# One ordinary GpSimd instruction behind the last 64-bit add of a launch

## The chip, the cores and the metric

One core of one Trainium2 chip. The metric is the device time of a launch in microseconds (us). The profiled span, from the first to the last instruction, is 1.7 to 1.9 us shorter than the device time of the same launch. Engines: PE is TensorE, PEld its weight loads, DVE VectorE, ACT ScalarE, POOL GpSimd, SP SyncE; a q behind the name is the engine's sequencer, under which waits, branches and library loads stand in the profile. The granted clock is TensorE's clock as a share of full speed. The chain is the work that ended last, followed back from the last instruction to what released it. An ACTIVATE is one ScalarE instruction. L1447 is line 1447 of that kernel's source; the changed kernel has one line more above this place and two above the end, so L1447 of before is L1448 of after.

## The reference, cut to what matters

```python
def reference(A_x, A_wq, A_wk, A_wv, A_wo, B_x, B_wqkv, B_w_phi, B_wo):
    # A: softmax attention, 32 query heads of 16, one key and value head, sequence 2048
    q = heads(A_x @ A_wq);  k = A_x @ A_wk;  v = A_x @ A_wv
    a = merge(softmax(q @ k.T * 16 ** -0.5) @ v) @ A_wo
    # B: linear attention with a softmax feature map, 32 heads of 16
    ...
    return concatenate([a, b], axis=-1)          # (1, 2048, 1024) bf16
```

## The kernel before, in the parts that matter

A scheduler in Python lays out a fixed order of instructions for every engine ahead of the launch. About two thirds of the exponentials of part A are ScalarE activations (L1646; 700 instructions of 1024 columns). The others (648 of 512 columns) are made from bits: VectorE scales scores into 16-bit words (L1751), and GpSimd makes shifted copies of four such words at a time with 64-bit adds (L1781):

```python
fn = lambda g: g.int64_add(out=b, in0=a, in1=256 * t * 0x1000100010001)
```

The start of the launch, cut:

```python
add("pool", lambda g: g.memset(self.ones, 1.0), writes=["ones"])
add("pool", lambda g: g.memset(self.zero, 0.0), writes=["zero"])
self.fill((512,) * self.NWARM, start=True)            # 12 warm-up matmuls on TensorE
last = self.load_xT(self.A_x, self.xT, 0, "AxT", None)  # first transposed chunk of x
...                                                   # loads of wk_raw, wq, wv; x chunks 1 to 3
add("pool", lambda g: g.memset(half[:, 0:1], 0.0), writes=["half0"])
...                                                   # four memsets of 16 rows of half
add("pool", lambda e: e.tensor_scalar(out=half[:, 1:2], in0=half[:, 0:1], scalar1=-1.0, scalar2=0.25,
                                      op0=ALU.mult, op1=ALU.add), reads=hk, writes=["half1"])      # L1447
add("pool", lambda g: g.tensor_copy(out=wk_rep..., in_=srck), reads=["wk_raw"], writes=["wk_rep"]) # L1450
...                                                   # memsets; the identity (affine_select, L1465); masks
```

The K projection (L1535) is the first real work of TensorE. It needs wk_rep and the first chunk of x. All GpSimd instructions run in this order. No library load is written in the source: the build puts one ahead of the first instruction that needs another library than the one known to be loaded. At the beginning of a launch it takes none as loaded, so there is a load ahead of L1447 and another ahead of the first 64-bit add. In the profile a load is a pair of MODIFY_POOL_CONFIG.

## Time and profile before

| | before |
|---|---|
| device time, median of 4 runs | 720.66 us (719.64 to 720.98) |
| profiled span (of one more launch, 721.12 us) | 719.37 us |
| busy: PE, DVE, ACT, POOL | 95, 86, 95, 72% |
| idle POOL ahead of the first tensor_scalar | 9.00 us |
| first ACTIVATE | 17.30 us |

The page cuts the span into 40 slices of 18 us and gives each a digit, the busy share in tenths.

```profile
PE   6999999999999999999999999999999999999995
...
ACT  1999999999999999999999999999999999999992
```

From the second slice on both are full. The prediction shows the lines of the first one.

### The profile page before, as it was taken

Reading aid. Unit: us, or ns where it says so; the run is one execution under the profiler, and the core shown is the slowest. Engines: PE = TensorE matmul, PEld = TensorE weight load, DVE = VectorE, ACT = ScalarE, POOL = GpSimd, SP = SyncE. Lnnn points to the kernel's source line nnn. Section 1 sums busy time; section 2 is a strip of 40 time slices with the busy share of each in tenths; the row PEclk is TensorE's granted clock in tenths of the full one; section 3 lists DMA queues with packets and bytes.
Section 4 is the critical chain, followed back from the end, with each engine's and each line's share of the span. In section 5 each row is a group of like instructions: output and inputs, shape, how many; then the busy total and the mean of one; then the engine's idle time right before and its main releaser. Section 6 shows DMA issues by size and latency. Waiting matters only on the chain.

```text
span 719.4 us, 18224 instructions
## 1 busy us (share of the span) xinstructions
PE 681.1 (95%) x7548; PEld 211.5 (29%) x7548; DVE 620.6 (86%) x1039; ACT 683.9 (95%) x771; POOL 521.4 (72%) x521
## 2 busy tenths in 40 slices
PE   6999999999999999999999999999999999999995
PEld 2322222322322332332222322323332323333322
DVE  1788899999999999999888988898978989889974
ACT  1999999999999999999999999999999999999992
POOL 3188788777777677776778878587878787777870
PEclk8999999999999999999999999999999999999999
DMA  6502233111112101111011111011111211111212
GB/s 139 127 3 39 42 38 66 19 7 12 9 13 37 9 8 10 14 9 10 7 8 19 16 20 17 12 19 23 20 17 9 28 22 23 16 14 16 31 16 52
DMA packets 47890, 18.28 MB, mean 25 GB/s; under 512 B 38708, under 2 KB 45940, under 8 KB 47800
## 3 DMA queue, kind: packets, MB, share of 16 engines
q1 hardware_dynamic: 45400, 16.23, 17.5%
q8 instruction: 60, 0.98, 0.6%
q10 hardware_dynamic: 2400, 0.82, 0.5%
q14 instruction: 30, 0.25, 0.1%
HBM read 2.28 MB, written 4.19 MB: 9 GB/s over the span
## 4 chain that ended last, share of the span: by engine, by line
ACT 49%; PE 30%; DVE 17%; issue 2%; POOL 1%; DMA 1%; SPq 0%; ACTq 0%; DVEq 0%; POOLq 0%
ACT f_PT L1646 47%; PE f_ps L1591 10%; DVE f_Z L1751 9%; PE f_ps L1811 8%; PE f_ps L1693 3%; PE f_ps L2245 2%; PE f_ps L1581 2%; PE f_ps L1897 1%; DVE f_vS L2103 1%; ACT f_ET L2160 1%; DVE f_ssum L2069 1%; PE f_ps L2153 1%; PE f_ps L2055 1%; DVE f_On L1878 1%; ACT f_Ek L2063 1%
## 5 line engine op out<-in xcount | busy, mean ns | idle before, releaser
L1646 ACT ACTIVATE f_PT<-f_ps 128x1024 bf16<-128x1024 f32 x700 | 654.8, 1093 | 20.5 <-PE f_ps L1591 17.8
L1781 POOL INT64_ADD f_Z<-f_Z x486 | 512.6, 1055 | 167.5 <-DVE f_Z L1751 128.5
L1751 DVE TENSOR_SCALAR f_Z<-f_ps 128x512 int16<-128x512 f32 x648 | 425.6, 681 | 53.6 <-PE f_ps L1591 50.9
L1591 PE MATMUL f_ps<-f_QA,f_KR 32*128 32x512 bf16 x2048 | 280.2, 384 | 15.1 <-ACT f_PT L1646 11.5
L1811 PE MATMUL f_ps<-f_Z,f_VK 128*32 128x512 f16 x2592 | 227.5, 386 | 4.2 <-DVE f_Z L1751 1.6
L1591 PEld LDWEIGHTS f_ps<-f_QA,f_KR 32*128 32x128 bf16 x2048 | 70.4, 91 | 254.7 <-ACT f_PT L1646 224.9
L1693 PE MATMUL f_ps<-f_PT,f_VA 128*32 128x512 bf16 x1400 | 131.6, 385 | 0.1
L1811 PEld LDWEIGHTS f_ps<-f_Z,f_VK 128*32 128x32 bf16 x2592 | 56.4, 94 | 105.4 <-issue 61.0
L1693 PEld LDWEIGHTS f_ps<-f_PT,f_VA 128*32 128x32 bf16 x1400 | 33.5, 94 | 47.8 <-issue 44.9
L2215 DVE TENSOR_TENSOR f_Wk<-f_ps,f_wq 128x512 bf16<-128x512 f32 x32 | 21.8, 680 | 3.6 <-PE f_ps L2204 3.6
L1412 PE MATMUL f_ps<-f_ones,f_zero 128*128 128x512 bf16 (+4 forms) x112 | 20.7, 369 | 1.3 <-POOL f_zero L1431 1.3
L1418 DVE COPY f_accS<-f_ps 128x512 f32<-128x512 f32 x31 | 21.0, 677 | 0.0
L1543 DVE TENSOR_SCALAR f_KR<-f_ps,f_half 128x512 bf16<-128x512 f32 x8 | 5.7, 744 | 17.7 <-PE f_ps L1535 17.7
L2103 DVE TENSOR_TENSOR f_vS<-f_ps,f_rs 128x1024 bf16<-128x1024 f32 x16 | 19.7, 1229 | 0.3 <-PE f_ps L2093 0.2
L2069 DVE TENSOR_REDUCE f_ssum<-f_Ek 128x64 f32<-128x1024 bf16 x16 | 19.3, 1204 | 0.0
L2160 ACT ACTIVATE f_ET<-f_ps 128x512 bf16<-128x512 f32 x32 | 18.8, 689 | 0.1
L2063 ACT ACTIVATE f_Ek<-f_ps 128x512 bf16<-128x512 f32 x32 | 18.2, 655 | 0.0
L1581 PE MATMUL f_ps<-f_AxT,f_wq 128*128 128x512 bf16 x64 | 17.7, 406 | 0.0
L2153 PE MATMUL f_ps<-f_BxT,f_Wq 128*128 128x512 bf16 x64 | 16.6, 382 | 0.7 <-DVE f_Z L1751 0.7
L2245 PE MATMUL f_ps<-f_Bwo,f_oT 128*128 128x512 bf16 x64 | 16.6, 382 | 0.4 <-DVE f_QA L1418 0.2
L1418 DVE CAST f_outB<-f_ps 128x512 bf16<-128x512 f32 x16 | 10.9, 681 | 6.8 <-PE f_ps L2245 6.8
L2055 PE MATMUL f_ps<-f_Wk,f_BxT 128*128 128x512 bf16 x64 | 16.6, 382 | 0.0
(94 smaller groups left out, 296.8 us busy)
## 6 DMA issues: line engine op xcount, KB each, us to landing
f_denS<-f_denS SPq DMA_DIRECT2D x124, 30.0 KB, 3.0
out_dram<-f_outB SPq DMA_DIRECT2D x16, 128.0 KB, 2.0
f_denC<-f_accS SPq DMA_DIRECT2D x124, 2.0 KB, 1.7
f_denS<-f_denC SPq DMA_DIRECT2D x124, 2.0 KB, 1.7
out_dram<-f_outA SPq DMA_DIRECT2D x14, 128.0 KB, 2.6
f_On<-f_Ot SPq DMA_DIRECT2D x60, 16.0 KB, 1.8
f_Bwv<-in_B_wqkv_dram SPq DMA_DIRECT2D x1, 512.0 KB, 4.5
f_Bwo<-in_B_wo_dram SPq DMA_DIRECT2D x1, 512.0 KB, 6.3
```

Source lines behind the costliest of these rows:

```text
L1418: self.add("dve", lambda v: v.tensor_copy(out=out, in_=in_), reads=reads, writes=writes)
L1581: mm = pe.matmul(ps[:, bank, :], lhsT=self.wq[:, dc, A * 128:A * 128 + 128], rhs=xT[:, dc, qc * 512:(qc + 1) * 512], start=(dc == 0), stop ...
L1591: return pe.matmul(self.ps[:, bank, :], lhsT=self.KR[32 * g:32 * g + 32, sc % 2, kap * 128:(kap + 1) * 128], rhs=self.QA[32 * g:32 * g + 3 ...
L1646: self.add("act", lambda a: a.activation(out=PT[:, sl[0]:sl[0] + size, :], in_=ps[:, b0:b0 + size, :], func=ACT.Exp), reads=[("PS", b0 + i ...
L1693: mm = pe.matmul(ps[32 * g:32 * g + 32, bank, :], lhsT=VA[:, kap, :], rhs=PT[:, slots[g], :], start=start, stop=stop, tile_position=(0, 32 ...
L1751: self.add("dve", lambda v: v.tensor_scalar(out=o, in0=ps[:, bank, :], scalar1=self.Z1, scalar2=self.Z0, op0=ALU.mult, op1=ALU.add), reads ...
L1781: fn = lambda g: g.int64_add(out=b, in0=a, in1=256 * t * 0x1000100010001)
L1811: mm = pe.matmul(ps[32 * g:32 * g + 32, bank, :], lhsT=self.VK[:, t, kap, :], rhs=Zf[:, sl[g], :], start=start, stop=stop, tile_position=( ...
L2069: self.add("dve", lambda v: v.tensor_reduce(out=ssum[:, r, :], in_=Ek[:, r].rearrange("p a h f -> p (a h) f"), axis=AX.X, op=ALU.add), rea ...
L2103: self.add("dve", lambda v: v.tensor_tensor(out=vS[:, :, :, 0:16], in0=v3, in1=rs.unsqueeze(3).to_broadcast([128, 2, 32, 16]), op=ALU.mult ...
L2160: self.add("act", lambda e: e.activation(out=self.ET[:, sl, :], in_=self.ps[:, bank, :], func=ACT.Exp, scale=1.0 - 2.0 * a), reads=[("PS", ...
L2245: mm = pe.matmul(ps[:, bank, :], lhsT=oT[:, r, C, :], rhs=self.Bwo[:, C, :], start=(C == 0), stop=(C == 3))
```

## The change

Intent: the launch shall end with the ordinary library loaded, so that the next launch of the same kernel finds it and its first load has nothing to do.

```diff
         self.half = sb("half", [128, 2], F32)
+        self.pad = sb("pad", [128, 1], F32)
...
         self.run()
+        self.add("pool", lambda g: g.tensor_scalar(out=self.pad, in0=self.half[:, 0:1], scalar1=1.0, scalar2=None, op0=ALU.mult), reads=["half1"], writes=["pad"])
         self.finish_last()
```

## The prediction

> **What bounds the kernel now.** I read the page first (shares of busy time, then the chain that ended last), then the chain and the waits of the first 20 us, then the GpSimd (POOL) timeline of the first 20 us and of the last 20, then the landings of the first loads. The page says that the body is bound by ScalarE and TensorE together:
>
> ```profile
> PE 681.1 (95%) x7548; PEld 211.5 (29%) x7548; DVE 620.6 (86%) x1039; ACT 683.9 (95%) x771; POOL 521.4 (72%) x521
> ...
> ACT 49%; PE 30%; DVE 17%; issue 2%; POOL 1%; DMA 1%; SPq 0%; ACTq 0%; DVEq 0%; POOLq 0%
> ```
>
> POOL has 28% of slack and is 1% of the chain that ended last, so one instruction more or less on it costs nothing in the body. The change can only matter at the two ends. At the start it is POOL that holds everything up. This is the timeline of POOL alone, in the first 12 us (start, us, instruction; in brackets the idle time before it):
>
> ```profile
> 1.31 0.10 POOL L1443 MEMSET f_half<- 128x1 f32 x1
> 1.47 0.54 POOL L1445 MEMSET f_half<- 16x1 f32 x4
> 11.01 0.18 POOL L1447 TENSOR_SCALAR f_half<-f_half 128x1 f32<-128x1 f32 x1 [9.00 <-issue]
> 11.34 0.61 POOL L1450 COPY f_wk_rep<-f_wk_raw 128x512 bf16<-128x512 bf16 x1 [0.15 <-POOL f_half L1447]
> ```
>
> A tensor_scalar on one element per partition waits 9.00 us for "issue", that is for nothing that the profile shows. The view of its source line shows what its sequencer ran just before, two pool reconfigurations at 2.0 to 2.1 us:
>
> ```profile
> L1447 POOLq MODIFY_POOL_CONFIG  x2: 2/2/2, 2.0 to 2.1; - x2
> ```
>
> The 64-bit add's line has the same pair at 20.6 us. So I read the 9 us as the loading of the ordinary library in the place of the 64-bit one, which the execution before had left. The chain carries this wait to the end of the kernel:
>
> ```profile
> 2.06 8.94 issue
> 11.01 0.19 POOL f_half L1447
> ...
> 11.34 0.62 POOL f_wk_rep L1450
> 11.96 0.09 issue
> 12.05 1.87 PE f_ps L1535 x4
> 13.92 3.02 PE f_ps L1581 x8
> 16.93 0.38 PE f_ps L1591 x4
> 17.32 53.45 ACT f_PT L1646 x58
> ```
>
> The K projection (L1535) needs wk_rep, the second POOL instruction behind the load. ScalarE, the bound, has done no ACTIVATE before 17.3 us. The waits of the same stretch give TensorE's share (us in total, times, longest):
>
> ```profile
> PE f_ps L1535 <- POOL f_wk_rep L1450: 5.6, 1, 5.6
> ```
>
> and the table of busy time by stretches (from:to, length, then each engine) has the granted clock in the third number from the end:
>
> ```profile
> 6.00:12.00 6.00, 0.45 (x2) 0.00 (x0) 0.00 (x0) 0.00 (x0) 0.79 (x2) 0.80 0.60 129
> 12.00:18.00 6.00, 5.95 (x34) 2.32 (x35) 3.09 (x5) 0.70 (x1) 5.14 (x14) 0.63 0.74 148
> ```
>
> TensorE stands still for 5.60 us, and while it does its granted clock falls (a mean of 0.80 and 0.63 in these two; 0.50 between 9.6 and 16.4 us in the clock records), so the first projections run at half speed.
>
> **What the Trainium skill says.** "GPSIMD Engine Reference", section Instruction dispatch: libraries of GpSimd code are put into instruction memory at run time, and the first call to a freshly loaded one pays about 6 us (5.95 measured there) "with no visible profile instruction". The trace agrees in kind: 8.94 us here, with the DMA engines busy. It does not say whether a load of what is already there is skipped, and that is the open question of this case. "Runtime: NRT & Kernel Launch", section `nrt_init` cost: a kernel on a runtime that is kept open starts from what the previous kernel left. That lets residency pass from launch to launch; no trace of before alone shows it. "TensorE: Matmul & The Clock Gate", Part 1: an idle window of some 3.4 us halves the clock. The trace agrees: 5.60 us idle, then 0.5 for 6.83 us.
>
> **The change part by part.** The order of instructions on TensorE, VectorE, ScalarE and the DMA queues is unchanged but for line numbers. On POOL there are two new rows behind the 486 adds: a library reload and a 128x1 tensor_scalar. The reload ahead of the first tensor_scalar of the launch stays in the program, and so does the one ahead of the first add. Nothing is removed: the whole gain has to come from the first reload having less to do.
>
> At the end: the last add finishes at 699.47 + 1.04 = 700.5 us. A load like the first (8.94) and a tensor_scalar (0.18) end at about 709.6. If the sequencer is held up too, its flag read, branch and drain follow, 699.4 to 703.8 in the trace of before, so 4.4 us: 714.0. The closing barrier falls at 719.2, as SyncE's drain comes at 719.1. Spare: 5 us. Cost on the path: 0, with perhaps 0.2 us if the load's reads slow the last stores.
>
> At the start, if the load is skipped or takes under 3 us:
> - half is done at 2.3 us. The copy to wk_rep then waits for wk_raw, whose landing is at 2.83 us: 2.9 + 0.61 = 3.5.
> - TensorE's K projection waits for the first x transpose, landed at 6.22, and for the warm-up matmuls that end at 1.31 + 5.14 = 6.45. It starts at 6.45 rather than at 12.05: 5.6 us.
> - With no idle stretch the clock stays at 1.0. The 12 matmuls of the chain took 1.87 + 3.02 = 4.89 us at half clock. Four such take 1.04 us with the full clock (L1535 at 18.70), eight by my estimate 1.8: 2.8 together, 2.1 us saved. ScalarE starts at about 17.3 - 7.7 = 9.6.
> - Are later loads then in time? x chunks land at 10.53, 14.74 and 19.21 us; their projections ran at 18.70, 24.24 and 27.96, so would run at 11.0, 16.5 and 20.3. All just in time, the first by half a microsecond. The adds' own load would be asked for at about 12 rather than 20.6, and be there at 21, before the first add's input (35.37 - 7.7 = 27.7). wphi (last landing 36.15) is first used at 66.9.
> - From 17.3 us the order is fixed and ScalarE runs 53 us without a break, so a shift of the start shifts all the rest. I keep 95% of it: 7.7 x 0.95 = 7.3 us, so 720.8 - 7.3 = 713.5.
>
> **The rivals.** (1) The load is skipped, 713.5 as above. For it: the intent of the change, and the kernel's own plan of its start. That plan sets the x chunks at 3.8, 8.6, 12.9 and 17.2 us, which is 1.8 to 2.4 below the landings of this trace, and wk_rep at 2.0, which is 10 below its end at 11.96. It also has just enough warm-up matmuls to reach 6.45. It looks drawn from runs in which wk_rep was not held up. (2) The pair of reconfigurations always unloads and loads, whatever is resident: the gap of 9.0 stays, and the added load lies in the shade of the tail: 720.9. For it: two instructions, not one, which looks like an unconditional take-out and put-in; and the program loads without asking at both places. (3) The state does not survive between executions (something between launches sets it anew): also 720.9. (4) The load is skipped but the next limit takes part of the gain: the first ScalarE work then meets the second x chunk at 10.53 or the clock still drops: 716. (5) The load at the end outlasts the tail: only if it took over 14 us; 722 to 726.
>
> **Range and chances.** Rivals 1 and 4 together I give 0.58, rivals 2 and 3 together 0.40, rival 5 0.02. The result has two humps, at 713.5 and at 720.9, with little between. I put the predicted time at 714.8, in the likelier hump and a little towards the other, and the range from 711.8 to 721.4 so that it holds both. 2% is 14.4 us; the whole POOL gap with all of the clock's loss is under 11.5, so faster by over 2% is nearly shut out (0.01), as is slower (0.01).
>
> **What would show it.** Right: the 9.00 ahead of the first tensor_scalar falls to under 3 us, TensorE's wait for wk_rep disappears, no stretch of clock 0.5 follows the warm-up, the first ACTIVATE is at 9 to 10.5 us, and the end moves by nearly as much. A new gap of some 9 us stands ahead of the tensor_scalar at about 701 to 710 us and nobody waits for it. Wrong: the 9.00 us stay at the start though the new tensor_scalar ran (rival 2 or 3); or the gap goes but ScalarE starts after 11 us (rival 4); or the closing barrier waits for POOL (rival 5).

## The result, and the profile after

713.00 us (712.58 to 713.43, 4 runs) against 720.66 us. The ratio of the two is 0.9896, 95% interval 0.9879 to 0.9913. All ratios here are the mean time of one kernel's fast runs over the mean of the other's of the same rounds (in the experiments the first launch of each kernel is left out), so not quite the quotient of the medians. The gain is real and small: 1.04%.

The timeline of POOL after the change, at the start and, after the dots, at the end:

```profile
1.47 0.54 POOL L1446 MEMSET f_half<- 16x1 f32 x4
2.31 0.18 POOL L1448 TENSOR_SCALAR f_half<-f_half 128x1 f32<-128x1 f32 x1 [0.31 <-POOL f_half L1446]
3.16 0.61 POOL L1451 COPY f_wk_rep<-f_wk_raw 128x512 bf16<-128x512 bf16 x1 [0.66 <-DMA f_wk_raw<-in_A_wk_dram]
...
689.13 3.31 POOL L1782 INT64_ADD f_Z<-f_Z  x3 [0.17 <-POOL f_Z L1782]
699.52 0.26 POOL L2302 TENSOR_SCALAR f_pad<-f_half 128x1 f32<-128x1 f32 x1 [7.08 <-DVE f_oT L1419]
```

The idle time ahead of the first tensor_scalar is down from 9.00 to 0.31 us, and the copy now waits for its data. The new gap of 7.08 us is at the end. Its releaser is named wrongly: the new instruction reads nothing that VectorE writes. VectorE's instruction only happens to end when the load does. The views of the two lines have the pair of reconfigurations at 2.2 us and at 692.5 us, right behind the last add:

```profile
L1448 POOLq MODIFY_POOL_CONFIG  x2: 2/2/2, 2.2 to 2.2; - x2
...
L2302 POOLq MODIFY_POOL_CONFIG  x2: 11/11/11, 692.5 to 692.5; - x2
```

The pair ahead of the first tensor_scalar is still in the program, and it still runs. It only costs nothing any more. "Skipped" is said of its time alone: the transfer of a library is in no DMA record, for the pages count the same 47890 packets and 18.28 MB with two loads to do (before) and with four (the run that leaves the 64-bit library, below). The chain of the first 30 us:

```profile
0.79 5.27 DMA f_AxT<-in_A_x_dram
6.06 0.07 issue
6.13 1.02 PE f_ps L1536 x4
7.16 1.73 PE f_ps L1582 x8
8.88 0.38 PE f_ps L1592 x4
9.27 21.31 ACT f_PT L1647 x23
```

GpSimd is gone from it. The first x chunk has taken its place as what TensorE waits for. The twelve projection matmuls take 1.02 + 1.73 = 2.75 us rather than 4.89. The table of stretches shows why:

```profile
6.00:12.00 6.00, 5.69 (x46) 2.38 (x47) 4.69 (x12) 2.75 (x3) 4.84 (x17) 1.00 0.59 128
12.00:18.00 6.00, 5.71 (x60) 1.92 (x60) 3.74 (x11) 6.00 (x8) 0.21 (x1) 1.00 0.74 139
```

The granted clock is 1.00 in both, against 0.80 and 0.63. ScalarE has done 2.75 us of ACTIVATEs by 12 us; before, it had done none.

Where did the time go after that? As the order is fixed, the n-th ACTIVATE of one kernel can be set against the n-th of another. This table has the start of an ACTIVATE minus that of the same one in before's profile, in us:

| ACTIVATE no. | its start before | after | 64-bit left | half on VectorE | 38 warm-up | after, 2 warm-up | the same again |
|---|---|---|---|---|---|---|---|
| 1 | 17.30 | -8.05 | -0.76 | -7.92 | -2.19 | -6.53 | -4.88 |
| 101 | 108.77 | -8.05 | -0.73 | -7.92 | -2.18 | -6.54 | -4.85 |
| 351 | 330.47 | -8.06 | -1.34 | -7.92 | -2.15 | -6.52 | -5.34 |
| 511 | 472.69 | -8.08 | -1.36 | -7.93 | -2.15 | -6.52 | -5.35 |
| 521 | 482.31 | -8.06 | -1.36 | -7.93 | -2.15 | -2.82 | -4.31 |
| 541 | 500.18 | -8.06 | -1.35 | -6.79 | +0.17 | -2.82 | -4.31 |
| 741 | 680.82 | -8.07 | -1.35 | -6.68 | +0.51 | -2.60 | -4.12 |

In this launch of the changed kernel the 8.05 us of the start arrive whole at 680 us. (The other columns are experiments, below.) Not every launch keeps all of it. When the changed kernel was run again, its profiled launch (714.08 us, the slowest of four) had 7.96 us at the first ACTIVATE and 6.68 at the 741st: from 489.2 us on its clock was halved for 3.41 us. The profiles with half on VectorE and with 38 warm-up matmuls lost time at the same place.

### The profile page after: what moved, and what is told of

It reads as the page before. It is cut to its first block, busy times and chain, and to the rows that moved or that the text cites. A ratio compares the mean times of both kernels' runs of the same rounds, so it can differ in the third digit from the quotient of the medians.

```text
span 711.0 us, 18172 instructions
## 1 busy us (share of the span) xinstructions
PE 669.8 (94%) x7493; PEld 211.0 (30%) x7548; DVE 620.6 (87%) x1039; ACT 683.7 (96%) x771; POOL 521.8 (73%) x522
## 2 busy tenths in 40 slices
DMA packets 47890, 18.28 MB, mean 26 GB/s; under 512 B 38708, under 2 KB 45940, under 8 KB 47800
## 4 chain that ended last, share of the span: by engine, by line
ACT 47%; PE 30%; DVE 20%; issue 1%; DMA 1%; POOL 1%; ACTq 0%; DVEq 0%
ACT f_PT L1647 45%; DVE f_Z L1752 11%; PE f_ps L1592 10%; PE f_ps L1812 8%; PE f_ps L1694 4%; PE f_ps L2246 2%; DVE f_ssum L2070 1%; DVE f_vS L2104 1%; ACT f_ET L2161 1%; PE f_ps L1582 1%; PE f_ps L1898 1%; DVE f_Wk L2216 1%; DMA f_AxT<-in_A_x_dram 1%; PE f_ps L2056 1%; DVE f_On L1879 1%
## 5 line engine op out<-in xcount | busy, mean ns | idle before, releaser
L2154 PE MATMUL f_ps<-f_BxT,f_Wq 128*128 128x512 bf16 x56 | 14.8, 381 | 1.9 <-issue 1.0
L2246 PE MATMUL f_ps<-f_Bwo,f_oT 128*128 128x512 bf16 x57 | 15.0, 381 | 1.5 <-issue 1.0
L2094 PE MATMUL f_ps<-f_Bwv,f_BxT 128*128 128x512 bf16 x56 | 15.0, 381 | 1.2 <-DVE f_Z L1752 0.8
L1879 DVE TENSOR_TENSOR f_On<-f_accS,f_denS 128x512 bf16<-128x512 f32 x16 | 15.3, 958 | 0.8 <-DMA f_denS<-f_denS 0.8
L2056 PE MATMUL f_ps<-f_Wk,f_BxT 128*128 128x512 bf16 x53 | 14.1, 380 | 1.8 <-issue 1.5
```

What stands on the lines that cost most here:

```text
L2246: mm = pe.matmul(ps[:, bank, :], lhsT=oT[:, r, C, :], rhs=self.Bwo[:, C, :], start=(C == 0), stop=(C == 3))
```

## The experiments

The theory: a load of the library that is already there is skipped, and what is there passes from launch to launch. The main rivals: any extra load or instruction at the end helps; only a call makes a library resident; a load is cheap at the start of a launch for some other reason; the gain needs the load to be gone, not only moved. Each run was timed against before in the same rounds. The medians of before in the three calls, each on another chip, were 721.06, 720.75 and 720.19 us.

### Leave the 64-bit library behind after all

The changed kernel with one tiny 64-bit add behind the new instruction:

```diff
+        p64 = [self.pad64[:, i, :].bitcast(I64) for i in range(2)]
+        self.add("pool", lambda g: g.memset(self.pad64[:, 0, :], 0), writes=["pad64a"])
+        self.add("pool", lambda g: g.int64_add(out=p64[1], in0=p64[0], in1=256), reads=["pad64a", "pad"], writes=["pad64"])
```

> The changed kernel with one more tiny 64-bit add behind the new tensor_scalar, so that the launch ends with the 64-bit library after all. Theory (a reload of the library that is already resident is skipped, and what is resident passes from launch to launch): the 9.0 us gap ahead of the first tensor_scalar is back, first ACTIVATE at 17.3 us, 720.7 us. Rival (any extra reload or ordinary instruction near the end helps, whatever is left resident): gap stays 0.3 us, 713.0 us. Both expect the two loads at the end to lie in the shade of the tail (some 7 us each, ending about 15 us after the last add of the body, close to the end).

Measured: 721.24 us (720.22 to 722.28), ratio 1.0008 (0.9987 to 1.0029). POOL at its start and end:

```profile
10.42 0.18 POOL L1449 TENSOR_SCALAR f_half<-f_half 128x1 f32<-128x1 f32 x1 [8.41 <-issue]
...
705.88 0.26 POOL L2303 TENSOR_SCALAR f_pad<-f_half 128x1 f32<-128x1 f32 x1 [6.71 <-issue]
706.20 0.10 POOL L2305 MEMSET f_pad<- 128x4 int16 x1
712.36 0.18 POOL L2306 INT64_ADD f_pad<-f_pad  x1 [6.05 <-issue]
```

The added tensor_scalar and its load run, the load takes 6.71 us, and still the gap at the start is 8.41 us, the first ACTIVATE at 16.53 us and the launch as long as before's. So it is not the extra work that helps but which library is left at the end. The two loads together end at 712.5 us, under a span of 718.5 us, and cost nothing either: the room at the end is larger than the prediction thought.

### A bare load, with nothing that uses it

The kernel before, with a load of the ordinary library in the place of the tensor_scalar:

```diff
         self.run()
+        self.add("pool", lambda g: g.load_library(standard))
         self.finish_last()
```

> The kernel before with a bare reload of the ordinary library at the end and no instruction behind it that uses it. If the reload itself makes the library resident: gap at the start 0.3 us and 713.0 us, as the changed kernel. If it takes a first call to bring the code in (the rival): gap near 9 us, or the part of it that the first call makes, and up to 720.7 us.

Measured: 713.73 us (712.83 to 714.07), ratio 0.9896 (0.9877 to 0.9915); first ACTIVATE at 9.57 us. POOL at the start:

```profile
2.33 0.18 POOL L1448 TENSOR_SCALAR f_half<-f_half 128x1 f32<-128x1 f32 x1 [0.32 <-POOL f_half L1446]
```

No call is needed. The tensor_scalar of the change is only the handle by which the build is made to put a load there.

### Two loads of one library in one launch

The kernel before, with a second load right behind the first tensor_scalar:

```diff
             reads=hk, writes=["half1"])
+        add("pool", lambda g: g.load_library(standard))
```

> The kernel before with a second reload of the ordinary library right behind the first tensor_scalar of the launch, ahead of the wk_rep copy. Theory (skip when resident): first gap 9.0 us as before, second gap about 0.3 us, 720.7 to 721.2 us. Rival (a reload is only cheap at the start of a launch, for another reason than residency): a second gap of 7 to 9 us, first ACTIVATE at 25 us, about 729 us.

Measured: 721.42 us (721.30 to 721.57), ratio 1.0006 (0.9989 to 1.0024); first ACTIVATE at 17.28 us.

```profile
10.36 0.18 POOL L1448 TENSOR_SCALAR f_half<-f_half 128x1 f32<-128x1 f32 x1 [8.35 <-issue]
11.05 0.61 POOL L1452 COPY f_wk_rep<-f_wk_raw 128x512 bf16<-128x512 bf16 x1 [0.51 <-POOLq L1450]
```

Two like pairs stand in one launch, 9 us apart. The first costs 8.35 us, the second 0.51. The skip has nothing to do with the start of a launch: it depends on what is loaded.

### Move the first tensor_scalar to VectorE

The kernel before, with the making of half on an engine that is idle then:

```diff
-        add("pool", lambda e: e.tensor_scalar(out=half[:, 1:2], in0=half[:, 0:1], scalar1=-1.0, scalar2=0.25, op0=ALU.mult, op1=ALU.add),
+        add("dve", lambda e: e.tensor_scalar(out=half[:, 1:2], in0=half[:, 0:1], scalar1=-1.0, scalar2=0.25, op0=ALU.mult, op1=ALU.add),
```

> The kernel before with the first tensor_scalar (half) moved from GpSimd to VectorE, which is idle then. The first instruction that needs the ordinary library is then the one that makes the identity, some 11 instructions later. Theory (the gain of the change is that wk_rep no longer waits for a load, nothing else): the load of 8 to 9 us moves to about 8 us from the start, off the path; first ACTIVATE at 9.3 us; 713.0 us, or up to 2 us more if the 64-bit library then comes too late for the first add (27.3 us). Rival (the gain needs the load to be gone altogether): 718 to 721 us.

Measured: 713.53 us (713.36 to 714.74), ratio 0.9895 (0.9878 to 0.9913); first ACTIVATE at 9.38 us.

```profile
2.99 0.61 POOL L1450 COPY f_wk_rep<-f_wk_raw 128x512 bf16<-128x512 bf16 x1 [0.98 <-DMA f_wk_raw<-in_A_wk_dram]
...
14.88 0.28 POOL L1465 TENSOR_SCALAR_AFFINE_SELECT f_ident<-f_ones 128x128 bf16<-128x128 bf16 x1 [7.20 <-issue]
...
27.45 3.31 POOL L1781 INT64_ADD f_Z<-f_Z  x3 [8.18 <-DVE f_Z L1751]
```

The load is not gone: 7.20 us of it stand ahead of the identity, where nobody waits. The memsets and the copy to wk_rep ran ahead of it, so they don't need the ordinary library. The 64-bit library, asked for at 19.5 us, is there in time too, for the first add waits for VectorE. The gain is the same as the change's, and as this launch pays its load off the path, it should not matter what ran on the core before (no run with another kernel ahead tests that).

### How much of the gain is the clock?

The 8.05 us are 12.05 - 6.13 = 5.92 us less waiting and 4.89 - 2.75 = 2.14 us less for the projections. Three runs try to get one part without the other. First the kernel before with longer warm-up (the edit is the same for 34):

```diff
-        self.fill((512,) * self.NWARM, start=True)
+        self.fill((512,) * 38, start=True)
```

> The kernel before with 38 instead of 12 warm-up matmuls, so that TensorE is busy until about 12 us and its clock does not fall while it waits for the load. My split of the 8.05 us by which the first ACTIVATE came earlier: 5.9 us of waiting and 2.1 us of half clock. If that holds: the gap of 8 to 9 us stays, no stretch of clock 0.5 between 9 and 17 us, the twelve projection matmuls take 2.8 instead of 4.9 us, first ACTIVATE at 15.2 us, 718.6 us. If the clock's share is nothing or is taken back: 720.7 us.

Measured: 719.55 us (719.02 to 721.43), ratio 0.9977 (0.9958 to 0.9996). The chain at the start:

```profile
1.31 10.55 PE f_ps L1412 x38
11.86 0.14 issue
12.00 1.02 PE f_ps L1535 x4
```

The start is as expected: the first ACTIVATE at 15.11 us, 2.19 earlier, with the K projection at full speed. The profiled run is at the same time the slowest of the four: it lost 2.7 us again some 490 us in (see the table above, and below). The others were at 719.02 to 719.62. As the warm-up itself now ended only at 11.86 us, I tried 34.

> As the run with 38 warm-up matmuls, with 34. With 38 the warm-up itself ended at 11.86 us and was the last thing that the K projection waited for, so a launch with a short load (8.3 us, wk_rep at 11.4) gained nothing by it. With 34 it ends at about 11.0. If that was why 38 gained 1.2 us in the median and not 2.1: first ACTIVATE at 14.6 to 15.1 us, 718.6 us. If the gain is limited by something else: 719.5 us again.

Measured: 719.49 us (718.07 to 721.00) against 720.19 us of before, ratio 1.0000 (0.9977 to 1.0022). The profile has the first ACTIVATE at 14.62 us and keeps the 2.7 us to the end, but the other three launches took 718.55 to 721.00 us. The size of the clock's part is shown at the start of the profiles: from the start of the K projection to the first ACTIVATE it is 5.25 us in before, 3.12 in the changed kernel, and 3.11 with 38 and with 34 warm-up matmuls, although the load's wait is still there. In the time of whole launches it drowns in the spread, and these two runs don't settle it.

Now the changed kernel with 2 warm-up matmuls, so that TensorE comes cold:

```diff
-        self.fill((512,) * self.NWARM, start=True)
+        self.fill((512,) * 2, start=True)
```

> The changed kernel with 2 instead of 12 warm-up matmuls: the load's wait stays away, but TensorE comes cold to the first projections. If the split holds: twelve projection matmuls in 4.9 instead of 2.8 us, first ACTIVATE at 11.4 us, 715.1 us. If the waiting alone made the gain: first ACTIVATE at 9.3 us, 713.0 us.

Measured: 717.94 us (717.50 to 718.34), ratio 0.9958 (0.9939 to 0.9977); first ACTIVATE at 10.76 us, earlier than expected, because the clock rose at 9.19 us, in the midst of the projections. But the launch took over 4 us more than the changed kernel, of which the start explains 1.4. So it was run again without a change.

> The changed kernel with 2 warm-up matmuls once more, unchanged. Its profile had the first ACTIVATE 1.4 us later than the changed kernel's of the same call, but lost another 3.7 us about 470 to 480 us in, where the clock was halved for 6.83 us after a stretch in which TensorE was busy 2.6 of 3.4 us. If that dip is chance from execution to execution: some runs at 714.9 to 715.3 us beside some at 717.5 to 718.5. If it belongs to this kernel: all at 717.5 to 718.5 us.

Measured: 716.87 us (715.54 to 718.39, 6 runs), ratio 0.9955 (0.9938 to 0.9973). Two of the six lie in the slower group, four between the groups, none in the faster one. This profile's first ACTIVATE is at 12.42 us, as here the projections ran at half clock to their end:

```profile
6.54 1.89 PE f_ps L1536 x4
8.43 3.41 PE f_ps L1582 x8
11.84 0.60 PE f_ps L1592 x4
```

So in these two profiles the first ACTIVATE comes 1.4 and 3.1 us later than in the changed kernel's repetition. The twelve projections took 4.25 and 5.30 us, by where the clock's rise falls; in the second the x chunk also landed 0.3 us later. Each then lost more at the same place of the body, 3.70 us in the first and 1.04 us in the second, between the 511th and the 521st ACTIVATE. One line of VectorE's timeline there differs, first the changed kernel's, then the first cold run's:

```profile
463.63 0.69 DVE L1879 TENSOR_TENSOR f_Ot<-f_accS,f_denS 128x512 bf16<-128x512 f32 x1 [0.15 <-DMA f_denS<-f_denS]
```

```profile
465.57 1.33 DVE L1879 TENSOR_TENSOR f_Ot<-f_accS,f_denS 128x512 bf16<-128x512 f32 x1 [0.54 <-DMA f_denS<-f_denS]
```

In the cold run it came while GpSimd's adds were running (from 465.32 us), and took twice as long. In the changed kernel it began just ahead of them. The stretch behind it then shows a clock that falls without TensorE ever being idle for long:

```profile
466.30:469.70 3.40, 2.62 (x29) 0.95 (x25) 3.40 (x6) 2.47 (x4) 2.43 (x3) 1.00 0.06 15
469.70:473.10 3.40, 3.25 (x27) 0.67 (x26) 2.68 (x5) 2.50 (x3) 2.32 (x3) 0.54 0.06 13
```

The second cold run had the slow instruction too (1.36 us), but no fall of the clock there. Such meetings are common: in each of the twelve profiles 13 to 16 of the 31 instructions of this VectorE line took over 0.9 us, and all of these started while an add was running (4 to 8 others started so too and were not slow). What the cold runs have is one more of them. Why the extra one came at that place is open, and so is what lets the clock fall. At the other place, some 490 us in, TensorE was busy for 2.53 of 3.41 us both in before (from 493.30 us) and in the changed kernel's repetition (from 485.35 us), and the granted clock of the next 3.41 us was 1.00 in before and 0.57 in the repetition.

What is shown is that a launch can lose time in the body whatever its start: 1.04 us where only the slow instruction was added, 3.70 where the clock fell too, and 1.25 to 2.66 where it fell some 490 us in. This is the noise in which the clock experiments drown.

### Is the first load of x slowed by the others?

As the chain of the changed kernel starts with that load, I kept 256 KB of other loads behind it, and took 10 warm-up matmuls:

```diff
-        S.dma1(... self.wq[:, :, 128:512], wqs[:, :, 128:512]), writes=[("wq", 1)], queue="act")
+        S.dma1(... self.wq[:, :, 128:256], wqs[:, :, 128:256]), writes=[("wq", 1)], queue="act")
         S.dma1(... self.wv ...)
+        S.dma1(... self.wq[:, :, 256:512], wqs[:, :, 256:512]), writes=[("wq", 2)], deps=[last], queue="act")
```

> The changed kernel where 256 KB of the query weights, which nothing needs before 40 us, are fetched only after the first x transpose has landed, and with 10 warm-up matmuls. The chain of the changed kernel now starts with that transpose (5.27 us to its landing at 6.06). If it is slowed by the other loads: landing at about 5.3 us, first ACTIVATE at 8.5 us, 712.3 us. If it takes its time alone: landing at 6.0 us, 713.0 us.

Measured: 713.78 us (713.10 to 715.28), ratio 0.9907 (0.9884 to 0.9929).

```profile
0.80 5.45 DMA f_AxT<-in_A_x_dram
6.25 0.02 issue
6.26 5.02 DMA f_AxT<-in_A_x_dram
```

Keeping these 256 KB back did not make the chunk faster: 5.45 us, against 5.27 (the other weights were still loaded beside it). The second chunk, which now had the delayed load beside it, landed at 11.28 us and held the second K projection up. This way gained nothing.

### The changed kernel again

> The changed kernel again on this chip, for comparison: 713.0 us, first ACTIVATE at 9.3 us, gap ahead of the first tensor_scalar 0.3 us.

Measured on the second of the three chips: 713.58 us (712.96 to 714.08), ratio 0.9894 (0.9875 to 0.9913), first ACTIVATE at 9.34 us, gap 0.31 us. The gain holds across chips and rounds. No version was found that clearly beats it; the bare load and the move to VectorE equal it.

## Why the prediction was right

- **The load is skipped when the library is there** (rival 1, given 0.58 with rival 4): right. 9.00 us became 0.31. It was argued from the kernel's own timetable, not seen, and at 0.58 it was little more than an even bet. The range, 711.8 to 721.4 us, took in both outcomes, so that the time fell into it says little; what counts is that this branch's steps came true one by one. One support was none: the prediction took the busy DMA engines as a sign of the load, but the load is in no DMA record, and their busy share from 2 to 6 us is 1.01 before and after. The two loads in one launch (8.35 and 0.51 us) show it directly, and the launch that leaves the 64-bit library (gap 8.41 us) shows that the state passes between launches. Rivals 2 and 3 fall, and with them the argument of rival 2: the pair of reconfigurations runs in both cases.
- **TensorE's wait**: 5.6 us expected, 5.92 measured. The chunk of x landed at 6.06 rather than 6.22, and the warm-up took 4.67 rather than 5.14 us, so it did not hold the projection up.
- **The clock's part**: 2.1 us expected, 2.14 measured in the chain.
- **First ACTIVATE**: 9.6 expected, 9.25 measured. The first 64-bit add came at 27.32 (expected 27.7).
- **What is kept to the end**: 95% expected, by feel. The table of ACTIVATEs says all in this launch, 8.05 us at the first and 8.07 at the 741st; the repetition's profile kept 84% (6.68 of 7.96). The medians moved by 7.66 us, the profiled spans by 8.35: before's profiled launch took 721.12 us, longer than any of the four timed ones. That 95% came close to the medians is in part luck.
- **The load at the end**: 8.9 us expected, 7.03 measured (692.49 to 699.52), and without cost as expected. The fear that it would hold up the sequencer was wrong: the flag was read while the load ran, and only the drain waited, from 697.0 for 2.88 us, until the tensor_scalar had ended at 699.8. That left 11 us to the closing barrier at 710.8, not 5.
- **The number on record**: 713.5 us for this branch against 713.00; the 714.8 on record lies above because it was drawn towards the other hump. The start gained 0.35 us more than the 7.7 expected, nearly all of it in TensorE's wait.

## What to carry to other kernels

Look at the first slice of a busy kernel for a tiny GpSimd instruction behind a long idle time that nothing releases, with a MODIFY_POOL_CONFIG pair ahead of it: that is a library load of 6 to 9 us. The sturdy cure is to let the first instruction that needs the library come late or run on another engine; leaving the right library behind at the end gains as much where the same kernel runs again, but a launch that follows something else may pay the load. Take the wait and the cold clock that follows it as one cost, and check how much of a shift at the start reaches the end by setting the n-th instruction of one trace against the n-th of the other.

## What the Trainium skill lacked or had wrong

- "GPSIMD Engine Reference", Instruction dispatch, has about 6 us for the first call to a freshly loaded library. Here a load took 8.3 to 8.9 us at the start of the launch, 7.20 behind the first loads, and 5.8 to 7.0 at the end. It lacks that a load of the resident library costs next to nothing (0.31 and 0.51 us of idle time in all), that a load's transfer is in no DMA record (47890 packets in every profile), and that the load needs no call: a bare one at the end left the next launch a gap of 0.32 us.
- "Runtime: NRT & Kernel Launch", `nrt_init` cost, says that a kernel starts from what the previous one left. It does not name the GpSimd library among it. The right one is worth 7.7 us of 720.7 here, and the gain goes when the launch leaves another one (721.24 us).
- "TensorE: Matmul & The Clock Gate", Part 1, ties the half clock to an idle window, and says further on that frequent short pauses can bring it too, but gives no amount. In the body of one run it fell, for 6.83 us, after 3.40 us in which TensorE was busy for 2.62; after 3.41 us with 2.53 busy it fell in one profile and not in another.
- "Perfetto Trace Analysis", GPSIMD Engine Instruction, warns of GpSimd spans. No page warns that the releaser of an idle time can be wrong when the true one is a library load: 7.08 us were put down to a VectorE instruction that the waiting one does not depend on.
